# Odd column counts in the additions of 1e-9, 80 partitions of queries and keys for nine heads, and values in one run a partition

## The chip, the cores and the metric

The kernel runs on one core of a Trainium2 chip. The metric is the device time of one execution in microseconds (us), over several runs; the profile is of one execution. The engines are TensorE (PE; PEld is its weight load), VectorE (DVE), ScalarE (ACT), GpSimd (POOL) and SyncE (SP), which issues nearly all DMA transfers here.

## What is computed

Blockwise causal attention of 4 batches, 8 heads, 576 positions and 64 columns a head (block 64), and on its result two feed-forward layers of 2304 tokens, 512 columns and 2048 hidden columns:

```python
scores = scale * np.matmul(q, k.transpose(0, 1, 3, 2))
mask = block_i >= block_j
scores = np.where(mask, scores, -1000000000.0)
scores = scores - np.max(scores, axis=-1, keepdims=True)
attn = np.exp(scores)
attn = attn / (np.sum(attn, axis=-1, keepdims=True) + 1e-09)
x = np.matmul(attn, v)                    # heads side by side: 2304 x 512
h = np.maximum(x @ w_in, 0.0);  x = h * h @ w_out
h = x @ w_in2                             # second layer
g = (a[0] + a[1]*h + a[2]*h**2 + a[3]*h**3) / (1 + abs(b[0])*abs(h) + abs(b[1])*h**2 + 1e-6)
out = g @ w_out2
```

## The kernel before

**Stages.** The program has one attention stage (some 355 us) with the first half of the first layer interleaved into it, then the second half of the first layer, then the second layer. Everything that the change touches lies in the attention stage. A head's 576 queries, padded to 640, are five tiles of 128 rows, in groups `GROUPS = ((0, 1), (2,), (3,), (4,))`. Heads 0 to 7 are visited twice, first for groups 0 and 1 (tiles 0 to 2), then for groups 2 and 3; the other 24 heads once for all four. Each (visit, group) is a slot. The loop at L589 goes through the slots and emits, for slot i: scores (`emit_s`, PE), the normalisation of slot i-1 (`emit_norm`), row maxima (`emit_max`, DVE), exponentials with row sums (`emit_exp`, ACT), the product with the values of slot i-4 (`emit_pv`), the transposes of slot i-3 (`emit_t`, PE, then copies by ACT and DVE), and pieces of the first layer (`moe_a`, through `advance`). Weight conversions (`Converter`, L89 to L129: ACT, DVE and POOL) are put between slots at a fixed pace. The tile framework tracks dependencies and orders the instructions of each engine with a planner that has costs of its own (`schedule_with_timeline_sim=True`, L891); the order in the trace therefore differs a little from the order of the text.

**Plain and split heads.** Heads 0 to 9 are plain (`PLAIN = 10`): they run in float32. The others are split into a high and a low part in float32r. A plain head's query and key arrays have 128 rows: rows 0 to 63 are the transposed head, rows 64 to 68 carry one mark for each tile, by which the score matmul adds the mask, and the rest are zeros. For a split head rows 64 to 127 repeat the head.

**Loads.** `load_qk` (L195) issues one query and one key transfer for each visit (two each for the first), up to four visits ahead; `qr` and `kr` have two buffers. `prep_qk` (L235) scales a plain head's queries on POOL (L239). `make_two` (L214), called at slot 36 with head 9's visit, copies rows 64 to 127 of its query and key tiles. `load_v` (L221) loads the values; two plain heads share a tile `vs` of 5 blocks of 128 columns, the even head in columns 0 to 63 of each block and the odd one in 64 to 127, so a transfer writes runs of 64 numbers (256 bytes) in each partition.

**Normalisation.** The row sums of plain heads lie in `sums`, a tile with two planes of two heads and 8 columns. After the odd head's group 1 (tiles 0 to 2) and group 3 (tiles 3 and 4) DVE adds 1e-9 (L351) for both heads at once, inverts (L352), and POOL spreads the result over 64 columns a head (`rb`, L355); PE transposes that (L447) and DVE multiplies (L449). For the split heads each slot has a tile `stat` (one of 8, 8 columns): negated maxima in columns 0 and 1, sums in 2 and 3, sums plus 1e-9 from 4 on (L362), inverses from 6 on (L363), and POOL multiplies the exponentials by them (L367). In the very first visit the maxima are scaled too (L331).

Of the kernel before, what the change touches and what calls it, by code (L numbers as in the profile page):

```python
# [8 lines left out]
F32 = mybir.dt.float32  # L9
# [3 lines left out]
ALU = mybir.AluOpType  # L13
# [4 lines left out]
P = 128  # L18
S = 576
SP = 640  # L20
D = 64
# [6 lines left out]
NB = 12  # L28
SCALE = 0.125
PLAIN = 10  # L30
SUBS = ((0, 320), (320, S))
SUB = 320
BLK = 512
# [16 lines left out]
def attention_moe_moe(ctx: ExitStack, tc: tile.TileContext, q, k, v, wi1, wo1, wi2, wo2, a, b, out):  # L50
    nc = tc.nc
# [84 lines left out]
    attn = tc.alloc_tile_pool(name="attn", bufs=1)  # L136
# [49 lines left out]
    class Visit:  # L186
        def __init__(self, n, hd, at, gis):
            self.n, self.hd, self.plain, self.at, self.gis = n, hd, hd < PLAIN, at, gis

            self.scale = SCALE if n == 0 else 1.0  # L190

            self.q0, self.q1 = (0, 3 * P) if gis == (0, 1) else (3 * P, SP) if gis == (2, 3) else (0, SP)
            self.k0, self.k1 = (D, D + SUB) if gis == (0, 1) else (0, S)

    def load_qk(un, eng=nc.sync):  # L195
        if len(un.gis) == 2 and un.n % 4 > 1:

            un.qr = f(attn.tile([P, SP], F32R, tag="qh", name=f"qr{un.n}", bufs=2))
            un.kr = f(attn.tile([P, S], F32R, tag="kk", name=f"kr{un.n}", bufs=2))
        else:  # L200
            un.qr = attn.tile([P, SP], F32, tag="qr", name=f"qr{un.n}", bufs=2)
            un.kr = attn.tile([P, S], F32, tag="kr", name=f"kr{un.n}", bufs=2)

        cuts = ((0, 256, D, 256), (256, un.q1, 256, un.k1)) if un.n == 0 else ((un.q0, un.q1, un.k0, un.k1),)
        for q0, q1, k0, k1 in cuts:
            nc.sync.dma_start(un.qr[:, q0:q1], q[un.hd][:, q0:q1])
            eng.dma_start(un.kr[:, k0:k1], k[un.hd][:, k0:k1])

# [10 lines left out]
    def load_v(un):  # L221
        src = v[un.hd].rearrange("p (c d) -> p c d", d=D)
        if un.plain:
            if un.hd % 2 == 0:
                un.vs = attn.tile([P, 5, P], F32, tag="vs", name=f"vs{un.n}", bufs=2)
            else:
                un.vs = units[un.n - 1].vs
            o = D * (un.hd % 2)
            nv = 3 if un.gis == (0, 1) else 5
            nc.sync.dma_start(un.vs[:, 0:nv, o:o + D], src[:, 0:nv])  # L230
        else:
            un.vr = attn.tile([P, 5, D], F32, tag="vr", name=f"vr{un.hd}", bufs=1)
            nc.sync.dma_start(un.vr, src)

    def prep_qk(un, step):  # L235
        if un.plain:
            if step == 0 and un.scale == 1.0:
                cols = un.qr[:, un.q0:un.q1]
                nc.gpsimd.tensor_scalar(cols, cols, SCALE, 0.0, op0=ALU.mult, op1=ALU.add)  # L239
            return  # L240
        if step == 0:
            hd = un.hd
            un.qh = attn.tile([P, SP], F32R, tag="qh", name=f"qh{hd}", bufs=2)
            un.kk = attn.tile([P, S], F32R, tag="kk", name=f"kk{hd}", bufs=2)
            nc.scalar.activation(un.qh, un.qr, AF.Copy, scale=SCALE)
            nc.scalar.activation(un.kk, un.kr, AF.Copy)
        else:
            un.q2, un.k2 = q_two[un.hd % 2], k_two[un.hd % 2]
            nc.vector.scalar_tensor_tensor(
                un.q2[0:D], un.qr[0:D], SCALE, f(un.qh[0:D]), op0=ALU.mult, op1=ALU.subtract)  # L250
            nc.gpsimd.tensor_tensor(un.kk[D:P], un.kr[D:P], f(un.kk[D:P]), op=ALU.subtract)
            nc.sync.dma_start(f(un.k2[0:D]), f(un.kk[0:D]))
# [11 lines left out]
    BANKS = {"mm": 2, "tp": 3, "sy": 1}  # L264


    sts = [attn.tile([P, 8], F32, name=f"stat{n}") for n in range(8)]
    for st in sts:
        nc.vector.memset(st, 1.0)

# [6 lines left out]
    def emit_s(i):  # L277
        un, gi = slots[i]
        g = GROUPS[gi]

        upper = un.gis == (0, 1)
        if un.hd % 2 and gi == 0 if upper else gi % 2:
            ps = ps1.tile([P, 2, 512], F32, tag="sx", name=f"sx{i}")
            if gi != 3:
                ps = ps[:, 0, :]
        else:
            tag = "mm" if upper and gi == 1 else "sy"
            ps = ps1.tile([P, 512], F32, tag=tag, name=f"sy{i}", bufs=BANKS[tag])
        spsum[i] = ps
        for t in g:  # L290

            cols = slice(P * t, P * (t + 1))
            if un.plain:
                products = [(un.qr[:, cols], un.kr)]
            else:
                products = [(un.qh[:, cols], un.kk), (un.q2[:, cols], un.k2)]
            w_ = P * t + D
            if t == 4:
                parts = [(ps[:, 0, 0:HS], 0, HS), (ps[:, 1, 0:HS], HS, S)]
            else:  # L300
                o = D if t == 1 else 0
                parts = [(ps[:, o:o + w_], D, D + w_)]
            for dst, lo, hi in parts:
                for z, (lhs, rhs) in enumerate(products):
                    last = nc.tensor.matmul(dst, lhs, rhs[:, lo:hi], start=z == 0, stop=z == len(products) - 1)
        marks.append(last)
# [13 lines left out]
    def emit_max(i):  # L320
        g = GROUPS[slots[i][1]]
        st = sts[i % len(sts)]
        stats[i] = st
        for n, t in enumerate(g):
            r = D if t == 0 else 0
            gates["max"] = nc.vector.tensor_reduce(st[r:P, n:n + 1], s_view(i, t), axis=AX.XY if t == 4 else AX.X,
                                    op=ALU.max, negate=True)
        un = slots[i][0]
        n = len(g)
        if un.plain and un.scale != 1.0:  # L330
            nc.vector.tensor_scalar(st[:, 0:n], st[:, 0:n], SCALE, None, op0=ALU.mult)  # L331

    def emit_exp(i):
        st = stats[i]
# [9 lines left out]
    def emit_norm(i):  # L344
        st = stats.pop(i)
        un, gi = slots[i]
        if un.plain:
            if un.hd % 2 and gi % 2:
                sm = sums[un.hd // 2 % 2]
                t0, t1 = TILES[gi // 2]  # L350
                nc.vector.tensor_scalar(sm[:, 1, :, t0:t1], sm[:, 0, :, t0:t1], 1e-9, None, op0=ALU.add)  # L351
                nc.vector.reciprocal(sm[:, 1, :, t0:t1], sm[:, 1, :, t0:t1])  # L352
                rb = attn.tile([P, t1 - t0, P], F32, tag="rb", name=f"rb{un.hd}_{gi}", bufs=2, padded_shape=[P, 3, P])
                for t in range(t0, t1):
# [4 lines left out]
            return  # L359
        g = GROUPS[slots[i][1]]  # L360
        n = len(g)
        nc.vector.tensor_scalar(st[:, 4:4 + n], st[:, 2:2 + n], 1e-9, None, op0=ALU.add)  # L362
        nc.vector.reciprocal(st[:, 6:6 + n], st[:, 4:4 + n])  # L363
        for n, t in enumerate(g):
            r = D if t == 0 else 0
            pv = ptile(slots[i][0], t)[r:P]
            nc.gpsimd.tensor_scalar(pv, pv, st[r:P, 6 + n:7 + n], 0.0, op0=ALU.mult, op1=ALU.add)  # L367

    def emit_t(i):
        nonlocal pt  # L370
# [52 lines left out]
    def emit_pv(un, half):  # L423
# [13 lines left out]
        if un.plain:  # L437
            for i, (c, src, dst, width) in enumerate(PV[half]):
                for n_, o in enumerate((0, D)):
                    nc.tensor.matmul(ps[o:o + D, dst:dst + width], un.vs[:, c, o:o + D],  # L440
                                     un.pt[:, n_, ROW[c], src:src + width],
                                     start=i == 0, stop=i == len(PV[half]) - 1)
            rb = spread.pop((hd, half))
# [451 lines left out]
```

## Time and profile before

| | |
|---|---|
| median of 3 runs | 1028.95 us (1028.33 to 1031.23) |
| profiled execution | 1030.96 us, of which its span, from the first to the last instruction, 1029.1 us |
| busy | PE 97%, PEld 86%, DVE 73%, ACT 71%, POOL 58% |
| mean granted TensorE clock | 0.996 |
| DMA | 106.59 MB in 63895 packets, 104 GB/s on average |

[...] A busy PE is one that has a matmul under way; where an engine stands, the wait is put down to what ended it. A share of the whole span says little about one stage, so the stages are read one by one.

### The profile page before, as it was taken

To read this page: it belongs to the slowest core of one execution; us is meant where nothing else is said; L and a number is where in the kernel's file an instruction comes from. 1 tells how busy PE (TensorE), PEld (TensorE's weight loads), DVE (VectorE), ACT (ScalarE), POOL (GpSimd) and SP (SyncE) were. 2 spreads that over 40 slices of the span, in tenths; PEclk is the share of its full clock that TensorE was granted. 3 is DMA by queue.
4 is the path that set the end of the run, shared out by engine and by line. 5 is a ranking of instruction groups with operands and counts; after the bars stand their busy time and mean duration, and the time that the engine had idled before them with its cause. 6 is when DMAs were issued, how large, how long until landed. Compare 5 with 4: busy or idle time off the path is not lost. (4 is left out here: it accounts for less than half of the span.)

```text
span 1029.1 us, 16981 instructions
## 1 busy us (share of the span) xinstructions
PE 993.8 (97%) x5657; PEld 880.1 (86%) x5657; DVE 754.5 (73%) x1436; ACT 732.1 (71%) x1650; POOL 594.3 (58%) x626
## 2 busy tenths in 40 slices
PE   6999998999999999899999999999999999999997
PEld 4668888999999999899788888887888888899996
DVE  6999588868787756677667765787766866776766
ACT  6798676868887755655465557777777777788775
POOL 4677785868687835531223447767455554755552
PEclk9999998999999999999999999999999999999999
DMA  8857434233323204457765473001101100110000
GB/s 282 251 173 235 117 106 150 75 109 104 118 86 86 74 21 128 164 181 231 234 221 182 136 259 123 1 1 41 42 1 31 41 1 1 32 41 1 31 1 32
DMA packets 63895, 106.59 MB, mean 104 GB/s; under 512 B 16064, under 2 KB 34496, under 8 KB 63808
## 3 DMA queue, kind: packets, MB, share of 16 engines
q1 hardware_dynamic: 63520, 105.34, 32.4%
q8 instruction: 45, 0.74, 0.3%
q14 instruction: 42, 0.34, 0.1%
q10 hardware_dynamic: 288, 0.16, 0.1%
HBM read 79.17 MB, written 23.07 MB: 99 GB/s over the span
## 5 line engine op out<-in xcount | busy, mean ns | idle before, releaser
L826 PE MATMUL yc<-w_co,gc 128*128 128x512 f32 x864 | 211.7, 391 | 2.9 <-ACT gc L786 2.9
L717 PE MATMUL hc<-xc,w_ci 128*128 128x512 f32 (+1 forms) x960 | 211.2, 368 | 0.0
L717 PEld LDWEIGHTS hc<-xc,w_ci 128*128 128x128 f32 x960 | 176.2, 188 | 26.2
L826 PEld LDWEIGHTS yc<-w_co,gc 128*128 128x128 f32 x864 | 161.3, 188 | 35.5 <-ACT gc L786 4.4
L787 POOL TENSOR_TENSOR gc<-t,gc 128x512 fp32r<-128x512 f32 (+1 forms) x78 | 105.1, 1354 | 126.3 <-issue 103.4
L493 PE MATMUL ha<-xt,w_ai 128*128 128x320 f32 (+1 forms) x768 | 123.3, 307 | 0.0
L506 PE MATMUL ya<-ga,w_ao 128*128 128x320 f32 (+1 forms) x768 | 117.7, 300 | 3.6 <-ACT r L519 2.2
L812 POOL TENSOR_TENSOR wq<-wq,ab 128x512 f32<-128x512 f32 (+1 forms) x78 | 96.3, 1235 | 28.4 <-ACT wq L810 28.4
L493 PEld LDWEIGHTS ha<-xt,w_ai 128*128 128x128 f32 x768 | 108.4, 191 | 4.7 <-issue 3.0
L506 PEld LDWEIGHTS ya<-ga,w_ao 128*128 128x128 f32 x768 | 106.4, 189 | 5.6 <-ACT r L519 2.4
L757 PE MATMUL yb<-gb,w_bo 128*128 128x512 f32 (+1 forms) x480 | 106.0, 368 | 2.2 <-DVE yp L762 2.0
L717 PE MATMUL hb<-xb,w_bi 128*128 128x512 f32 (+1 forms) x480 | 105.8, 368 | 0.1
L757 PEld LDWEIGHTS yb<-gb,w_bo 128*128 128x128 f32 x480 | 87.6, 188 | 14.2 <-ACT gb L520 2.4
L813 DVE TENSOR_TENSOR t<-hc,t 128x512 f32<-128x512 f32 (+1 forms) x80 | 50.9, 636 | 65.9 <-ACT t L811 65.9
L786 ACT ACTIVATE gc<-t 128x512 fp32r<-128x512 f32 (+1 forms) x80 | 47.1, 589 | 72.9 <-DVE t L795 72.9
L717 PEld LDWEIGHTS hb<-xb,w_bi 128*128 128x128 f32 x480 | 87.4, 188 | 11.6 <-ACT yo L511 0.5
L367 POOL TENSOR_SCALAR p<-p,stat 64x64 f32<-64x64 f32 (+4 forms) x110 | 61.9, 567 | 37.5 <-DVE stat L363 11.7
L387 PE MATMUL tp<-ident,p 128*128 128x128 f32 x416 | 74.4, 286 | 7.0 <-DVE pt L413 4.1
L793 DVE SCALAR_TENSOR_TENSOR wq<-wq,ab 128x512 f32<-128x512 f32 (+1 forms) x80 | 55.0, 687 | 33.8 <-ACT ab L792 22.7
L413 DVE TENSOR_TENSOR pt<-tp,pt 64x64 fp32r<-64x64 f32 (+2 forms) x198 | 64.1, 343 | 19.5 <-ACT pt L411 16.5
L411 ACT ACTIVATE pt<-tp 64x64 fp32r<-64x64 f32 (+2 forms) x198 | 58.2, 320 | 21.6 <-PE tp L387 18.7
L795 DVE SCALAR_TENSOR_TENSOR t<-t,coef,ab 128x512 f32<-128x512 f32 (+1 forms) x80 | 66.8, 835 | 1.7
(140 smaller groups left out, 2006.3 us busy)
## 6 DMA issues: line engine op xcount, KB each, us to landing
kr<-in_k_dram SPq DMA_DIRECT2D x32, 288.0 KB, 3.8
raw_ci<-in_wi_dram SPq DMA_DIRECT2D x16, 512.0 KB, 4.3
raw_co<-in_wo_dram SPq DMA_DIRECT2D x16, 512.0 KB, 4.1
qr<-in_q_dram SPq DMA_DIRECT2D x24, 320.0 KB, 3.2
raw_ai<-in_wi_dram SPq DMA_DIRECT2D x8, 512.0 KB, 4.9
raw_ao<-in_wo_dram SPq DMA_DIRECT2D x8, 512.0 KB, 4.2
raw_bi<-in_wi_dram SPq DMA_DIRECT2D x8, 512.0 KB, 3.7
raw_bo<-in_wo_dram SPq DMA_DIRECT2D x8, 512.0 KB, 3.9
```

The source lines that it names most:

```text
L367: nc.gpsimd.tensor_scalar(pv, pv, st[r:P, 6 + n:7 + n], 0.0, op0=ALU.mult, op1=ALU.add)
L387: nc.tensor.transpose(ps[:, P * n:P * (n + 1)], pblock(un, t, c), ident)
L411: nc.scalar.activation(high, src, AF.Copy)
L413: nc.vector.tensor_tensor(low_, src, f(high), op=ALU.subtract)
L493: nc.tensor.matmul(ps[:, 0:n], w[:, zw, P * kk:P * (kk + 1)], xt[:, zx, kk, first:end], start=i == 0, stop=i == 3 * KK - 1)
L506: nc.tensor.matmul(ps[:, 0:n], wA["o", m][:, zw, P * c:P * (c + 1)], gs[m][:, zg, 0:n], start=i == 0, stop=i == 3 * HALF - 1)
L717: nc.tensor.matmul(ps[:, 0:n], w[:, zw, P * kk:P * (kk + 1)], xt[:, zx, kk, 0:n], start=i == 0, stop=i == 3 * KK - 1)
L757: nc.tensor.matmul(acc[j, c][:, 0:n], wB["o", m][:, zw, P * c:P * (c + 1)], g[:, zg, 0:n], start=m == 0 and i == 0, stop=last and i == 2)
L787: (nc.vector if u - 2 >= len(units) - END else nc.gpsimd).tensor_tensor(g[:, 1, 0:n], t, f(g[:, 0, 0:n]), op=ALU.subtract)
L795: nc.vector.scalar_tensor_tensor(t, t, a0, r, op0=ALU.add, op1=ALU.mult)
L812: (nc.vector if u >= len(units) - END else nc.gpsimd).tensor_tensor(w, w, ab, op=ALU.mult)
L826: last = nc.tensor.matmul(acc[j, c], g[:, zg, P * c:P * (c + 1)], w3["o", m][:, zw, :], start=m == 0 and i == 0, stop=m == NM - 1 and i == 2)
```

## The change

Four edits, all in the attention stage.

1. Additions of 1e-9 and the first scaling get odd column counts. L351 becomes two instructions of three columns, one for each head of the pair, always the last three columns of the half (0 to 2 or 2 to 4; column 2 is added to twice). L362 covers 2n - 1 columns for a group of n tiles: one for one, three for two; the tile `stat` grows from 8 to 11 columns and the inverses move to column 8. L331 is issued once for each column.
2. Heads 0 to 8 load, scale and use 80 partitions of queries and keys (`kp`) in place of 128. Head 9 keeps 128, since `make_two` reads its upper rows.
3. The values of two plain heads lie one head after the other in `vs`, so that each transfer writes one run of 768 or 1280 bytes in a partition.
4. The matmuls of scores and values follow these layouts.

```diff
--- before.py
+++ after.py
@@ -28,6 +28,7 @@
 NB = 12
 SCALE = 0.125
 PLAIN = 10
+KPLAIN = 80
 SUBS = ((0, 320), (320, S))
 SUB = 320
 BLK = 512
@@ -188,6 +189,7 @@
             self.n, self.hd, self.plain, self.at, self.gis = n, hd, hd < PLAIN, at, gis
 
             self.scale = SCALE if n == 0 else 1.0
+            self.kp = KPLAIN if hd < PLAIN - 1 else P
 
             self.q0, self.q1 = (0, 3 * P) if gis == (0, 1) else (3 * P, SP) if gis == (2, 3) else (0, SP)
             self.k0, self.k1 = (D, D + SUB) if gis == (0, 1) else (0, S)
@@ -203,8 +205,8 @@
 
         cuts = ((0, 256, D, 256), (256, un.q1, 256, un.k1)) if un.n == 0 else ((un.q0, un.q1, un.k0, un.k1),)
         for q0, q1, k0, k1 in cuts:
-            nc.sync.dma_start(un.qr[:, q0:q1], q[un.hd][:, q0:q1])
-            eng.dma_start(un.kr[:, k0:k1], k[un.hd][:, k0:k1])
+            nc.sync.dma_start(un.qr[0:un.kp, q0:q1], q[un.hd][0:un.kp, q0:q1])
+            eng.dma_start(un.kr[0:un.kp, k0:k1], k[un.hd][0:un.kp, k0:k1])
 
 
 
@@ -222,12 +224,11 @@
         src = v[un.hd].rearrange("p (c d) -> p c d", d=D)
         if un.plain:
             if un.hd % 2 == 0:
-                un.vs = attn.tile([P, 5, P], F32, tag="vs", name=f"vs{un.n}", bufs=2)
+                un.vs = attn.tile([P, 2, 5, D], F32, tag="vs", name=f"vs{un.n}", bufs=2)
             else:
                 un.vs = units[un.n - 1].vs
-            o = D * (un.hd % 2)
             nv = 3 if un.gis == (0, 1) else 5
-            nc.sync.dma_start(un.vs[:, 0:nv, o:o + D], src[:, 0:nv])
+            nc.sync.dma_start(un.vs[:, un.hd % 2, 0:nv], src[:, 0:nv])
         else:
             un.vr = attn.tile([P, 5, D], F32, tag="vr", name=f"vr{un.hd}", bufs=1)
             nc.sync.dma_start(un.vr, src)
@@ -235,7 +236,7 @@
     def prep_qk(un, step):
         if un.plain:
             if step == 0 and un.scale == 1.0:
-                cols = un.qr[:, un.q0:un.q1]
+                cols = un.qr[0:un.kp, un.q0:un.q1]
                 nc.gpsimd.tensor_scalar(cols, cols, SCALE, 0.0, op0=ALU.mult, op1=ALU.add)
             return
         if step == 0:
@@ -264,7 +265,7 @@
     BANKS = {"mm": 2, "tp": 3, "sy": 1}
 
 
-    sts = [attn.tile([P, 8], F32, name=f"stat{n}") for n in range(8)]
+    sts = [attn.tile([P, 11], F32, name=f"stat{n}") for n in range(8)]
     for st in sts:
         nc.vector.memset(st, 1.0)
 
@@ -291,7 +292,7 @@
 
             cols = slice(P * t, P * (t + 1))
             if un.plain:
-                products = [(un.qr[:, cols], un.kr)]
+                products = [(un.qr[0:un.kp, cols], un.kr[0:un.kp])]
             else:
                 products = [(un.qh[:, cols], un.kk), (un.q2[:, cols], un.k2)]
             w_ = P * t + D
@@ -328,7 +329,8 @@
         un = slots[i][0]
         n = len(g)
         if un.plain and un.scale != 1.0:
-            nc.vector.tensor_scalar(st[:, 0:n], st[:, 0:n], SCALE, None, op0=ALU.mult)
+            for c in range(n):
+                nc.vector.tensor_scalar(st[:, c:c + 1], st[:, c:c + 1], SCALE, None, op0=ALU.mult)
 
     def emit_exp(i):
         st = stats[i]
@@ -348,7 +350,8 @@
             if un.hd % 2 and gi % 2:
                 sm = sums[un.hd // 2 % 2]
                 t0, t1 = TILES[gi // 2]
-                nc.vector.tensor_scalar(sm[:, 1, :, t0:t1], sm[:, 0, :, t0:t1], 1e-9, None, op0=ALU.add)
+                for n_ in range(2):
+                    nc.vector.tensor_scalar(sm[:, 1, n_, t1 - 3:t1], sm[:, 0, n_, t1 - 3:t1], 1e-9, None, op0=ALU.add)
                 nc.vector.reciprocal(sm[:, 1, :, t0:t1], sm[:, 1, :, t0:t1])
                 rb = attn.tile([P, t1 - t0, P], F32, tag="rb", name=f"rb{un.hd}_{gi}", bufs=2, padded_shape=[P, 3, P])
                 for t in range(t0, t1):
@@ -359,12 +362,13 @@
             return
         g = GROUPS[slots[i][1]]
         n = len(g)
-        nc.vector.tensor_scalar(st[:, 4:4 + n], st[:, 2:2 + n], 1e-9, None, op0=ALU.add)
-        nc.vector.reciprocal(st[:, 6:6 + n], st[:, 4:4 + n])
+        w_ = 2 * n - 1
+        nc.vector.tensor_scalar(st[:, 5:5 + w_], st[:, 2:2 + w_], 1e-9, None, op0=ALU.add)
+        nc.vector.reciprocal(st[:, 8:8 + n], st[:, 5:5 + n])
         for n, t in enumerate(g):
             r = D if t == 0 else 0
             pv = ptile(slots[i][0], t)[r:P]
-            nc.gpsimd.tensor_scalar(pv, pv, st[r:P, 6 + n:7 + n], 0.0, op0=ALU.mult, op1=ALU.add)
+            nc.gpsimd.tensor_scalar(pv, pv, st[r:P, 8 + n:9 + n], 0.0, op0=ALU.mult, op1=ALU.add)
 
     def emit_t(i):
         nonlocal pt
@@ -437,7 +441,7 @@
         if un.plain:
             for i, (c, src, dst, width) in enumerate(PV[half]):
                 for n_, o in enumerate((0, D)):
-                    nc.tensor.matmul(ps[o:o + D, dst:dst + width], un.vs[:, c, o:o + D],
+                    nc.tensor.matmul(ps[o:o + D, dst:dst + width], un.vs[:, n_, c],
                                      un.pt[:, n_, ROW[c], src:src + width],
                                      start=i == 0, stop=i == len(PV[half]) - 1)
             rb = spread.pop((hd, half))
```

## Rows read from the trace of the kernel before

**Rows 1.** Page, busy us, share of the span and instructions of each engine.
```profile
PE 993.8 (97%) x5657; PEld 880.1 (86%) x5657; DVE 754.5 (73%) x1436; ACT 732.1 (71%) x1650; POOL 594.3 (58%) x626
```

**Rows 2.** Stages: length, busy PE, PEld, DVE, ACT, POOL, clock, DMA share, GB/s.
```profile
0.00:25.00 25.00, 17.11 (x85) 12.13 (x86) 15.66 (x53) 16.81 (x60) 11.57 (x32) 1.00 0.89 280
25.00:100.00 75.00, 70.09 (x427) 53.16 (x424) 70.03 (x120) 63.19 (x184) 52.54 (x67) 1.00 0.72 220
100.00:360.00 260.00, 252.07 (x1920) 244.63 (x1919) 199.22 (x585) 198.47 (x603) 195.30 (x269) 0.99 0.36 104
```

**Rows 3.** PE's waits, 0 to 25 us: us in total, times, longest.
```profile
PE sy L305 <- DMA kr<-in_k_dram: 3.7, 1, 3.7
PE sx L305 <- DMA kr<-in_k_dram: 1.5, 1, 1.5
```

**Rows 4.** PE's waits, 100 to 360 us.
```profile
PE tp L387 <- DVE pt L413: 3.7, 4, 2.7
...
PE pv L453 <- DVE pt L413: 1.0, 1, 1.0
```

**Rows 5.** DVE groups by form, whole span: busy us, mean ns | idle before.
```profile
L362 DVE TENSOR_SCALAR stat<-stat 128x1 f32<-128x1 f32 x66 | 9.8, 149 | 12.4 <-ACT p L339 11.3 <-ACT ga L520 0.2
...
L362 DVE TENSOR_SCALAR stat<-stat 128x2 f32<-128x2 f32 x22 | 8.6, 390 | 8.9 <-ACT p L339 8.8
...
L351 DVE TENSOR_SCALAR sums<-sums 128x6 f32<-128x6 f32 x5 | 2.8, 560 | 0.0
...
L351 DVE TENSOR_SCALAR sums<-sums 128x4 f32<-128x4 f32 x5 | 1.1, 215 | 0.4 <-ACT p L339 0.4
...
L331 DVE TENSOR_SCALAR stat<-stat 128x2 f32<-128x2 f32 x1 | 0.5, 475 | 0.0
...
L331 DVE TENSOR_SCALAR stat<-stat 128x1 f32<-128x1 f32 x1 | 0.2, 154 | 0.0
```

**Rows 6.** In order of time, from 86.5 us: start, us, engine, line, operation [idle before].
```profile
86.80 1.69 POOL L251 TENSOR_TENSOR kk<-kr,kk 64x576 fp32r<-64x576 f32 x1 [2.55 <-ACT kk L246]
...
87.14 1.38 DVE L351 TENSOR_SCALAR sums<-sums 128x6 f32<-128x6 f32 x1
```

**Rows 7.** In order of time, the first 30 us.
```profile
2.13 0.43 SPq L207 DMA_DIRECT2D kr<-in_k_dram  x1
...
5.71 0.51 POOL L239 TENSOR_SCALAR qr<-qr 128x384 f32<-128x384 f32 x1 [3.00 <-DMA qr<-in_q_dram]
5.77 0.47 DVE L331 TENSOR_SCALAR stat<-stat 128x2 f32<-128x2 f32 x1
...
7.64 1.41 PE L305 MATMUL sx<-kr,qr 128*128 128x64 f32 x4 [1.48 <-DMA kr<-in_k_dram]
```

**Rows 8.** In order of time, from 165 to 176 us.
```profile
167.79 0.15 DVE L362 TENSOR_SCALAR stat<-stat 128x2 f32<-128x2 f32 x1
...
175.22 0.47 PE L387 MATMUL tp<-ident,p 128*128 128x128 f32 x1 [2.65 <-DVE pt L413]
```

**Rows 9.** PE groups by form, 0 to 105 us.
```profile
L305 PE MATMUL sy<-kr,qr 128*128 128x320 f32 x16 | 6.8, 510 | 0.0
...
L305 PE MATMUL sy<-kr,qr 128*128 128x64 f32 x12 | 2.4, 286 | 4.0 <-DMA kr<-in_k_dram 3.7 <-issue 0.3
```

**Rows 10.** Stretches with the k_two copy alone, and with early loads; columns as rows 2.
```profile
139.20:140.00 0.80, 0.80 (x9) 0.80 (x8) 0.80 (x2) 0.80 (x4) 0.80 (x1) 1.00 0.80 184
3.00:5.00 2.00, 1.31 (x5) 1.34 (x6) 0.00 (x0) 0.00 (x0) 0.00 (x0) 1.00 0.73 179
9.00:12.00 3.00, 3.00 (x15) 2.30 (x14) 2.33 (x7) 2.15 (x10) 0.51 (x1) 1.00 1.06 386
```

**Rows 11.** Page, DMA packets of the whole span.
```profile
DMA packets 63895, 106.59 MB, mean 104 GB/s; under 512 B 16064, under 2 KB 34496, under 8 KB 63808
```

**Rows 12.** The stretch of the lower clock; columns as rows 2.
```profile
174.00:183.00 9.00, 7.76 (x37) 7.50 (x38) 6.81 (x25) 4.26 (x15) 2.47 (x5) 0.62 0.54 188
```

## Prediction

> **What bounds the kernel now.** I read the page's busy times first: TensorE (PE) is busy 993.8 of 1029.1 us [rows 1], so no edit can win more than the 35 us in which it stands, and only where it stands. The busy times by stage [rows 2] show where: 7.9 us in the first 25, 4.9 in the next 75, 7.9 from 100 to 360. The reader is to see two things there. From 25 to 100 VectorE (DVE) is as full as PE (70.0 and 70.1 of 75 us), so what DVE does there can delay PE. From 100 to 360 DVE has 61 us free, and extra DVE time mostly fills idle time. The first 25 us are neither.
>
> Who ended PE's waits says what they are. At the start they are mainly two loads, 3.7 and 1.5 us [rows 3]. From 100 to 360 PE waits 4.7 us for DVE in five waits, 2.7 us of it in one [rows 4].
>
> The page and the windows are of one execution, of 1030.96 us with a span of 1029.1, so 1.9 us lie around the span. The median of the runs shown is 1028.95, 2.0 lower. I sum against the execution and carry the difference over to the median.
>
> **The additions.** In one-column form L362 takes 149 ns (66 times), in two-column form 390 (22 times). The sums at L351 average 560 ns with six columns and 215 with four; L331 takes 475 with two and 154 with one [rows 5]. The excess is not work. The six-column addition at 87.14 ends at 88.52, 0.03 us after GpSimd's (POOL's) L251 ends at 88.49 [rows 6]; the two-column L331 at 5.77 ends at 6.24, POOL's L239 at 6.22 [rows 7]. So an operation with an even number of columns waits for the POOL instruction that is running. With POOL idle it does not, as L362 at 167.79 with 150 ns shows [rows 8].
>
> After the change L362 has three columns (or one), L351 is two instructions of three, L331 two of one. No row has an odd count above one. The bounds are the one-column rows (149 ns) and the even rows of the same line (L351: 3.9 us over 10, 390 ns; L362: 390). I take the free price, because only even counts are slow in the rows, but only just; the other is a rival. Then:
> - L362: 22 x (390 - 149) = 5.3 us of DVE saved from 100 on. On the path that is between 0 and the 4.7 us that PE waits for DVE there [rows 4]. Without the one long wait, before which the last two-column addition already takes 150 ns [rows 8], 2.0 are left; I take half, 1.0.
> - L351: 3.9 us now, 20 x 0.149 = 3.0 after, 0.9 saved. It belongs to the plain heads, so to the stage up to 100, where DVE is full; but PE is idle only 4.9 us there [rows 2], and I count half a microsecond for each of DVE's: 0.45. If they wait: 20 x 0.39 = 7.8, so 3.9 lost.
> - L331: 0.63 us becomes 3 x 0.149 = 0.45. I count nothing, since PE's next matmul waits for a load until 7.64 [rows 7]. Where that load is early, 0.2.
>
> The addition of the second half now also rewrites column 2, which the first half's rb copies (L355 on POOL) read. That is a new wait of DVE for POOL, behind which every later DVE instruction would queue. It costs nothing while those copies are two slots old; if they are late, one POOL instruction.
>
> [...]
>
> **Queries and keys, 80 rows.** The number of transfers stays, and none is moved on SP's queue; three eighths of the bytes of the first nine heads go. For each of eight heads that is 768 KB before, for head 8 it is 608: 6752 x 3/8 = 2532 KB, 2.6 MB. Scaling L239 on POOL (0.51 us, [rows 7]) and the score matmuls keep their columns. A matmul's time goes with its columns, 510 ns for 320 and 286 for 64 [rows 9]; no row has fewer contraction rows, so the bounds are 0 and 3/8 of each, and I take 0.
>
> What of the loads is on the path? PE stands 1.48 us until the second unit's keys, issued at 2.13, have landed at about 7.6 [rows 7]. That much can be won there and no more, because the third unit's loads are queued right behind. Of the 3.7 before the first matmul [rows 3] only a small part is transfer: 224 KB at the 386 GB/s of 9 to 12 us [rows 10] are 0.6 us, 3/8 of that 0.2. Bounds 0 to 1.5 and 0 to 0.2; I take 0.7 and 0.2. Later loads are hidden by the matmuls of the units before them: PE names no load after the second unit [rows 3]. Without that cover a key load of 288 KB would give 108 KB at 386 GB/s, 0.3 us.
>
> Against it speaks a transfer of 64 rows in this trace, the k_two copy: alone it moved 184 GB/s with the DMA engines 0.80 busy, while full-height loads from 9 to 12 us moved 386 at 1.06 [rows 10]. Per byte 64 rows cost 1.6 times the engine time, so half the rows cost 0.8 of it, and 80 rows save a fifth at most. For it speaks that the first loads move only 179 GB/s from 3 to 5 us [rows 10]: there the engines' rate is not the limit, and five rows for each of them end sooner than eight. So I take half of the bound.
>
> [...]
>
> **Values.** The 18 loads have 8 x 384 + 10 x 640 = 9472 packets of 256 bytes, of the 16064 that are under 512 [rows 11]; after the change they are 18 x 128 = 2304 larger ones. That frees DMA time, but no wait in rows 3 names a value load: 0, at most 0.2 for the queries behind them.
>
> **Sum.** 0.2 + 0.7 + 0.45 + 1.0 = 2.35 us: 1028.6 against the profiled execution, 1026.6 against the median.
>
> **Rivals.**
> - *The loads don't shrink.* For it the 64-row copy, against it the slow first loads [rows 10]. Then 0.45 + 1.0 are left: 1027.5.
> - *Three columns still wait.* For it every slow row has two columns or more, against it none is odd [rows 5]. L351 loses between 10 x 0.149 = 1.5 and 3.9, say 2.7, half of it on the path; L362 wins 0, the loads 0.9: 0.45 slower, 1029.4.
> [...]
> [...]
>
> **How the numbers follow.** A measurement of this kernel can tell some 0.3% from no change, 3.1 us: under 1025.9 is faster, over 1032.0 slower. Chances: forecast 0.36 (its own range 1024.5 to 1028.6), no shrinking 0.14, still waiting 0.22, stall gone 0.16, new stall 0.12. Faster: 0.14 of the forecast, 0.04, 0.02 and 0.16, together 0.36. Slower: 0.11 of the new stall and 0.03 of the waiting case, 0.14. Same 0.50. The range runs from 1021.0, through the case without the stall, to 1031.5, which takes in the full 3.9 us of waiting sums; the new stall and half of the case without the old one lie outside, 0.2.
>
> **What would show it.** L362 in three columns at 150 ns, and twenty L351 at 150, confirm the first step; 390 refutes it. The second unit's matmul before 7.6 confirms the load term; an unchanged start refutes it. 104.0 MB and some 6600 packets under 512 bytes show that the edits act. [...]

## The result and the profile after

| | before | after |
|---|---|---|
| median | 1029.12 us (1027.62 to 1031.23) | 1039.07 us (1038.10 to 1042.24) |
| ratio | | 1.0099, 95% interval 1.0080 to 1.0117 |
| profiled execution, span | 1030.96, 1029.1 us | 1038.99, 1037.2 us |
| mean granted TensorE clock | 0.996 | 0.993 |

The change makes the kernel 10 us slower, and 1026.6 was forecast. Ratios, here and below, compare runs in the fast state alone; one run of a later kernel, `e1_full_rows` with 2507.41 us, was not in it. The page of the changed kernel has busy times and packets, to be read beside [rows 1, 11]; then come the stages of [rows 2] with the same columns (length, busy PE, PEld, DVE, ACT, POOL, the granted share of TensorE's full clock, the mean busy share of the 16 DMA engines, GB/s).

```profile
PE 1003.4 (97%) x5657; PEld 886.7 (85%) x5657; DVE 756.7 (73%) x1447; ACT 732.8 (71%) x1650; POOL 593.5 (57%) x626
...
DMA packets 55000, 104.00 MB, mean 100 GB/s; under 512 B 6593, under 2 KB 26081, under 8 KB 54913
```

```profile
0.00:25.00 25.00, 21.51 (x77) 16.18 (x77) 15.51 (x52) 14.97 (x53) 10.12 (x33) 1.00 0.76 228
25.00:100.00 75.00, 67.80 (x380) 48.54 (x381) 63.44 (x115) 59.44 (x175) 44.50 (x59) 0.95 0.57 178
100.00:360.00 260.00, 249.58 (x1888) 241.98 (x1886) 202.79 (x582) 198.08 (x599) 194.78 (x263) 0.99 0.37 109
```

TensorE is busy 9.6 us longer with the same 5657 matmuls, and it does fewer of them early: 77 in the first 25 us where there were 85 [rows 2], though it is busy 21.5 us and not 17.1. Matmuls became slower, not more. The loads did what the diff says (104.0 MB, 6593 small packets).

Where the slowness lies is read from one form of matmul in two stretches, the first up to 22 us, the second behind it (busy us, mean ns | idle before).

```profile
L306 PE MATMUL sy<-kr,qr 80*128 80x320 f32 x11 | 6.8, 714 | 0.0
L391 PE MATMUL tp<-ident,p 128*128 128x128 f32 x12 | 3.2, 426 | 0.0
```

```profile
L306 PE MATMUL sy<-kr,qr 80*128 80x320 f32 x6 | 2.2, 452 | 1.6 <-ACT p L341 1.6
L391 PE MATMUL tp<-ident,p 128*128 128x128 f32 x8 | 1.2, 273 | 0.0
```

The same forms take 1.6 times as long before 22 us, the transposes too, which the change does not touch. That is a lower clock level, and the trace's records of the granted clock say the same: their first entry of the full level (1.00) is at 10.7 us before and at 22.0 after. The level up to 22 us is that of the stretch below, 0.50: 192 columns of the product with the values (L444) take 541 ns from 3 to 22 us and 541 ns from 28.9 to 35.5. (The views by stretch print 1.00 ahead of that first entry, so there the durations have to be read.) And the clock falls once more, from 28.8 to 35.6:

```profile
22.00:28.80 6.80, 4.60 (x25) 3.00 (x23) 5.25 (x12) 3.49 (x13) 4.31 (x8) 1.00 0.59 160
28.80:35.60 6.80, 6.28 (x21) 3.76 (x20) 5.02 (x9) 4.93 (x19) 2.29 (x4) 0.50 0.54 156
```

Before that fall TensorE stood 2.2 of 6.8 us. Its longest wait there can be followed back in order of time (start, us, engine, line):

```profile
24.02 2.50 DVE L123 SCALAR_TENSOR_TENSOR cv_ai<-cv_ai,raw_ai 128x512 uint32<-128x512 uint32 x1
...
26.44 0.48 DVE L327 TENSOR_REDUCE stat<-sy 128x1 f32<-128x320 f32 x1
...
26.96 0.53 ACT L341 ACTIVATE p<-sy,stat 128x320 f32<-128x320 f32 x1 [1.83 <-DVE stat L327]
...
27.63 0.81 PE L306 MATMUL sy<-kr,qr 80*128 80x320 f32 x2 [1.62 <-ACT p L341]
```

A conversion of 2.50 us on DVE delays a row maximum, that the exponential, that TensorE.

As a milestone I take the first matmul of the first feed-forward layer, the same instruction in every kernel: at 38.66 us before and at 46.13 after, 7.5 later. Where these 7.5 us come from is seen by the exponentials (each tile of scores has one, in the same order in both kernels). The 5th starts 2.4 us earlier than before (7.82 instead of 10.19 us), the 17th 1.0 us later (24.61 instead of 23.61), the 28th 6.8 us later (45.82 instead of 38.99). So the slow start eats the lead that the loads had given and one microsecond more, and most of the loss at the milestone comes behind it, in and after the half-clock stretch from 28.8. 10.3 us are lost at the layer's 151st matmul (120.97 instead of 110.65 us), 8.0 at the last matmul of the kernel.

### The profile page after: what moved, and what is told of

It reads as the page before. It is cut to its first block, busy times and chain, and to the rows that moved or that the text cites. A ratio compares the mean times of both kernels' runs of the same rounds, so it can differ in the third digit from the quotient of the medians.

```text
span 1037.2 us, 16996 instructions
## 1 busy us (share of the span) xinstructions
PE 1003.4 (97%) x5657; PEld 886.7 (85%) x5657; DVE 756.7 (73%) x1447; ACT 732.8 (71%) x1650; POOL 593.5 (57%) x626
## 2 busy tenths in 40 slices
DMA packets 55000, 104.00 MB, mean 100 GB/s; under 512 B 6593, under 2 KB 26081, under 8 KB 54913
## 5 line engine op out<-in xcount | busy, mean ns | idle before, releaser
L830 PEld LDWEIGHTS yc<-w_co,gc 128*128 128x128 f32 x864 | 161.3, 188 | 35.6 <-ACT gc L790 4.5
L816 POOL TENSOR_TENSOR wq<-wq,ab 128x512 f32<-128x512 f32 (+1 forms) x78 | 96.4, 1236 | 28.7 <-ACT wq L814 28.6
```

The lines of the kernel that those rows point to most:

```text
L816: (nc.vector if u >= len(units) - END else nc.gpsimd).tensor_tensor(w, w, ab, op=ALU.mult)
L830: last = nc.tensor.matmul(acc[j, c], g[:, zg, P * c:P * (c + 1)], w3["o", m][:, zw, :], start=m == 0 and i == 0, stop=m == NM - 1 and i == 2)
```

## The experiments

Theory 1: score matmuls of 80 rows keep TensorE at its lower clock. Theory 2: the earlier loads, or the new order that the planner makes of everything, cost the time. Theory 3: the additions do. The table has all kernels; the clock columns come from the records of the granted clock in each trace, the milestone from its instructions. Each ratio is to the kernel before in runs on the same chip, where its median was 1028.63 to 1029.82 us; it need not be the quotient of two medians. Clock and milestone are of one profiled execution of each kernel.

| kernel | score rows | median us | ratio, 95% interval | full clock first at | half again, up to 100 us | milestone |
|---|---|---|---|---|---|---|
| before | 128 | 1029.12 | 1 | 10.7 | none | 38.66 |
| after | 80 | 1039.07 | 1.0099 (1.0080 to 1.0117) | 22.0 | 28.8 to 35.6 | 46.13 |
| e1_full_rows | 128 | 1028.78 | 0.9992 (0.9973 to 1.0010) | 10.9 | 96.2 to 103.0 | 36.30 |
| e2_matmul_rows | 80 | 1039.16 | 1.0069 (1.0033 to 1.0105) | 38.0 | none | 46.93 |
| e3_edit2 | 80 | 1030.61 | 1.0012 (0.9987 to 1.0036) | 22.0 | 73.2 to 76.6 | 39.22 |
| e4_load_rows | 128 | 1029.11 | 0.9994 (0.9975 to 1.0013) | 6.8 | 10.2 to 17.0, 34.1 to 37.5 | 41.83 |
| text_before | 128 | 1059.58 | 1.0306 (1.0279 to 1.0333) | 12.1 | none | 38.99 |
| text_matmul | 80 | 1067.64 | 1.0379 (1.0362 to 1.0396) | 23.9 | 27.3 to 34.1 | 46.10 |
| text_after_full | 128 | 1060.92 | 1.0314 (1.0292 to 1.0336) | 10.3 | none | 38.42 |
| text_after | 80 | 1063.23 | 1.0336 (1.0318 to 1.0355) | 23.6 | none | 43.80 |
| matmul_96 | 96 | 1031.40 | 1.0024 (1.0011 to 1.0037) | 12.2 | 25.8 to 32.6 | 40.34 |
| single_columns | 128 | 1025.65 | 0.9974 (0.9956 to 0.9993) | 10.9 | none | 38.16 |
| combined | 128 | 1030.46 | 1.0016 (1.0003 to 1.0030) | 7.7 | 28.2 to 31.6 | 38.20 |
| combined_warm | 128 | 1028.86 | 1.0002 (0.9989 to 1.0015) | 5.9 | none | 34.92 |
| after_old_additions | 80 | 1039.56 | 1.0096 (1.0071 to 1.0121) | 21.7 | 28.6 to 35.4, 76.3 to 79.8 | 46.44 |
| after_old_values | 80 | 1034.95 | 1.0058 (1.0035 to 1.0081) | 13.8 | 37.7 to 41.1 | 39.11 |
| after_warm | 80 | 1049.26 | 1.0193 (1.0168 to 1.0218) | 6.1 | four stretches | 49.41 |
| single_warm | 128 | 1029.86 | 1.0013 (1.0001 to 1.0025) | 6.4 | 67.9 to 71.3 | 36.56 |

### The change taken apart

**All but the rows.** The changed kernel with 128 rows:

```diff
-KPLAIN = 80
+KPLAIN = 128
```

> The changed kernel with its 80 rows set back to 128: loads, scalings of the queries and score matmuls of the first nine heads are of 128 rows again, the three-column additions and the values in one run stay. Theory 1 (score matmuls of 80 rows keep TensorE at its lower clock): the granted clock reaches full at about 10 to 11 us, as in the kernel before, the only later stretch at half is the one near 175 us, and the time is 1028 to 1031 us. Theory 2 (the changed order or the earlier loads keep it low): the loads are those of before, so 1028 to 1031 us as well if the loads do it, but about 1038 us if the order that comes with the additions does it. Theory 3 (the additions, which wait beside GpSimd as before and are twice as many in the running sums): 1037 to 1040 us.

The loss is gone: 1028.78 us. Its 128x320 matmuls between 11 and 22 us are at full clock:

```profile
L306 PE MATMUL sy<-kr,qr 128*128 128x320 f32 x10 | 3.6, 439 | 0.0
```

So theory 3 falls: additions and values cost nothing that shows here. The clock did not do all that theory 1 expected: besides the stretch near 175 us it is at half from 96.2 to 103.0 us and twice behind 250 us, and the time is that of the kernel before all the same.

**The matmuls alone.** On the kernel before:

```diff
-                products = [(un.qr[:, cols], un.kr)]
+                products = [(un.qr[0:un.kp, cols], un.kr[0:un.kp])]
```

> The kernel before with one thing changed: the score matmuls of the first nine heads read 80 rows of queries and keys instead of 128 (loads, scalings, additions and values as before). Theory 1: the granted clock is at half until 18 us or later and falls again within the first 40 us; the time is 1036 to 1041 us. Theories 2 and 3: the clock rises at about 10 to 11 us and the time stays at 1027 to 1031 us. The prediction's own term for this step was 0 us.

1039.16 us, by the ratio 7 us (3 to 11) more than before. The fall expected within 40 us did not come, since the clock first rises at 38.0. From 12 to 38 us TensorE has not a gap, and its matmuls still take the time of the lower level (first the two stretches, columns as in the stages above, then a form from 12 to 38 us):

```profile
12.00:38.00 26.00, 26.00 (x83) 17.52 (x82) 13.76 (x38) 16.29 (x60) 12.11 (x22) 1.00 0.73 212
38.00:50.00 12.00, 11.30 (x58) 7.17 (x57) 10.41 (x20) 9.68 (x31) 8.59 (x13) 1.00 0.73 227
```

```profile
L307 PE MATMUL sy<-kr,qr 80*128 80x320 f32 x12 | 7.6, 741 | 0.0
```

So busy time alone did not bring the full level here: TensorE was busy for 26.00 of 26.00 us, and a score matmul of 320 columns still took 741 ns, where `e1_full_rows` above has 439 at the full level.

**The whole of edit 2, and the loads alone.** `e3_edit2` is the kernel before with the diff's loads, scaling and score matmuls of 80 rows. `e4_load_rows` loads 96 rows but keeps matmuls of 128, over rows that VectorE has set to zero:

```diff
+                nc.vector.memset(t[96:P], 0.0)
+                nc.vector.memset(u[96:P], 0.0)
```

> The kernel before with the whole of the second edit: loads, scalings and score matmuls of 80 rows for the first nine heads; additions and values as before. Theory 1: as with the matmuls alone, less the microsecond that the earlier loads give: 1035 to 1040 us, full clock first after 18 us or later. Theory 2 (the loads): the same, so that only the kernels with the matmuls alone and with the loads alone tell these two apart. Theory 3 (additions): 1027 to 1030 us.

> The kernel before with short loads alone: 96 rows of queries and keys are loaded for the first nine heads, rows 96 to 127 of the four pairs of buffers are set to zero once by VectorE, and the score matmuls keep 128 rows. Theory 1: the granted clock reaches full at 9 to 12 us and the time is that of the kernel before or 1 to 2 us less, 1026 to 1029.5 us. Theory 2 (loads that land sooner put the work into an order that keeps the clock low): 1035 us or more. The prediction's load terms (0.2 + 0.7 us) are seen here alone: second unit's first score matmul before 7.2 us instead of 7.64.

The loads alone change nothing in the time that can be measured (0.9994), as theory 1 has it. The second unit's first matmul comes at 5.62 us, as expected (before 7.2), but the eight settings to zero (4.5 us of DVE up to 6.4 us) put the first exponential at 8.26 us instead of 6.34, so what the loads are worth in time is not seen alone here. The clock is full at 6.8 us, sooner than expected, and lost again at 10.2 behind a wait of 2.1 us. The second edit whole was a miss of theory 1: full clock at 22.0 us, as in the changed kernel, and yet 1030.61 us. In its trace no fall follows the rise before 73.2 us, and the 28th exponential starts at 39.57 us where the kernel before has it at 38.99 and the changed kernel at 45.82. From 25 to 100 us VectorE is nearly full in the kernel before (70.0 of 75 us [rows 2]), so TensorE may be able to make up a late start there, if no second fall comes; no run tests that by itself. With 80 rows the clock comes late; what that costs differs from kernel to kernel. Since every kernel so far also had its own order from the planner, this needed a test in which the order stands still.

### The same order on every engine

The planner is switched off in four kernels, so that each engine runs the order of the text:

```diff
-    with tile.TileContext(nc, schedule_with_timeline_sim=True) as tc:
+    with tile.TileContext(nc, schedule_with_timeline_sim=False) as tc:
```

`text_before` and `text_matmul` (the matmul edit above) then have instruction for instruction the same order on all engines, as have `text_after_full` and `text_after`.

> The kernel before with its planner switched off: each engine runs its instructions in the order of the text. It is the baseline of three more kernels with the same order, so that a difference between them is not one of order. Its own time is not known; no theory names it, and somewhat more than 1029 us is likely. What counts is its granted clock in the first 60 us: with score matmuls of 128 rows theory 1 expects full clock from 10 to 13 us.

> The same order of the text, with the score matmuls of the first nine heads reading 80 rows: every engine has the same instructions in the same order as in the baseline, and only these matmuls differ. Theory 1 (the rows keep the clock low): full clock later than in the baseline by 8 us or more, and a time 3 to 10 us above it. Theory 2 (the new order of the planner is what cost the time): the clock as in the baseline and a time within 2 us of it.

> The changed kernel in the order of the text, with its 80 rows set back to 128: against the baseline it has the additions and the layout of the values alone. Theories 1 and 2: within 2 us of the baseline, since the additions move work of VectorE by less than 4 us in all. Theory 3 (the additions cost the time): 5 us or more above it.

> The changed kernel as it is in the order of the text; its engines have the same instructions in the same order as the kernel with 128 rows beside it, and loads, scalings and score matmuls have 80. Theory 1: full clock later by 8 us or more and 3 to 10 us more than that kernel. Theory 2: no more time than that kernel, since the order is the same and the loads are shorter, 0 to 2 us less.

`text_matmul` takes 8.1 us more than `text_before` (1067.64 against 1059.58, and the intervals of the ratios stay apart). The form of its score matmuls from 12.2 to 23.6 us, first of the baseline, then with 80 rows:

```profile
L305 PE MATMUL sy<-kr,qr 128*128 128x320 f32 x8 | 3.2, 482 | 0.0
...
L305 PE MATMUL sx<-kr,qr 128*128 128x192 f32 x4 | 1.1, 354 | 0.0
```

```profile
L305 PE MATMUL sy<-kr,qr 80*128 80x320 f32 x6 | 3.8, 742 | 0.0
...
L305 PE MATMUL sx<-kr,qr 80*128 80x192 f32 x4 | 1.9, 581 | 0.0
```

And stretches of both, in the same order:

```profile
12.00:24.00 12.00, 9.36 (x55) 6.43 (x54) 10.86 (x27) 10.69 (x41) 8.39 (x14) 1.00 0.77 225
24.00:27.30 3.30, 3.30 (x24) 2.37 (x23) 3.24 (x9) 2.75 (x10) 1.69 (x3) 1.00 0.84 231
27.30:34.10 6.80, 6.15 (x29) 3.27 (x27) 5.92 (x14) 6.69 (x24) 5.87 (x12) 1.00 0.76 213
```

```profile
12.00:24.00 12.00, 12.00 (x41) 8.17 (x40) 6.63 (x16) 6.09 (x22) 4.74 (x7) 1.00 0.52 163
24.00:27.30 3.30, 1.66 (x11) 1.12 (x9) 2.84 (x7) 3.20 (x14) 2.22 (x3) 1.00 0.39 79
27.30:34.10 6.80, 6.24 (x20) 4.32 (x20) 4.66 (x12) 3.90 (x15) 3.44 (x7) 0.50 0.70 240
```

From 12 to 24 us the baseline does 55 matmuls in 9.36 us; the kernel with 80 rows does 41 and is busy for all 12.00. It loses 4.9 us there (at the 13th exponential), 2.3 more in the half-clock stretch behind it (at the 20th), and is 7.1 us late at the milestone. Theory 2 can't explain that: nothing in the order differs. In these two kernels the difference shrinks to 5.1 us at the end of the attention and grows to 9.3 in the second layer by further half-clock stretches; those I don't ascribe to the rows. So of the 8.1 us some 5 can be followed to the start; whether the rest belongs to the rows is open.

The fall at 27.3 us stands beside a wait of TensorE for a scaling of queries on POOL (L239): 2.20 us, ended at 27.86. The kernel with 128 rows has the same wait at the same instruction, 2.21 us, ended at 22.95, and stays at full clock.

`text_after` agrees on the clock (23.6 against 10.3 us) and at the milestone (5.4 us later than `text_after_full`), but no fall follows its rise, and its median is only 2.3 us above, short of the 3 expected; the intervals of these two overlap.

### How many rows, one addition, and what is left

`matmul_96` reads 96 rows (the matmul edit with 96), `single_columns` takes the wait out of the split heads' addition:

```diff
-        nc.vector.tensor_scalar(st[:, 4:4 + n], st[:, 2:2 + n], 1e-9, None, op0=ALU.add)
+        for c in range(n):
+            nc.vector.tensor_scalar(st[:, 4 + c:5 + c], st[:, 2 + c:3 + c], 1e-9, None, op0=ALU.add)
```

> The kernel before with the score matmuls of the first nine heads reading 96 rows instead of 128 (80 cost 7 us). If the loss grows with the rows left out, 96 rows lose less than 80: full clock between 11 and 24 us and 1029 to 1036 us. If it is a matter of any missing row, about 1036 us.

> The kernel before with the two-column addition of 1e-9 to the sums of the split heads (390 ns) issued as two additions of one column, nothing else. This measures the prediction's second term alone, 1.0 us of gain: the single columns at about 150 ns each, 300 in place of 390 a slot, and a time of 1027 to 1030 us. A rival: two instructions take DVE as much as one that waits, and the time stays within 0.5 us of the kernel before.

With 96 rows 2.5 us are lost (0.24%), less than with 80: the full level comes at 12.2 us, but a half-clock stretch follows at 25.8. The single columns are the one kernel that beats both, 1025.65 us, 0.7 to 4.5 us less than before; 1027 to 1030 was expected. All 110 take the price of one column:

```profile
L363 DVE TENSOR_SCALAR stat<-stat 128x1 f32<-128x1 f32 x110 | 15.9, 149 | 20.6 <-ACT p L339 20.1
```

The longest wait of [rows 4] stays in it, with 2.7 us, so the gain does not come from there. Which waits gave it was not traced further, and the planner's order is another one here too, so that the gain is not shown to be that of the additions alone.

`combined` puts the useful parts together, and `combined_warm` adds work for TensorE ahead of the first load:

```diff
+    warm = attn.tile([P, SUB], F32, tag="tmp", name="warm", bufs=2)
+    nc.vector.memset(warm, 0.0)
+    for n in range(3):
+        ps = ps1.tile([P, 512], F32, tag="mm", name=f"warm{n}", bufs=2)
+        nc.tensor.matmul(ps[:, 0:SUB], warm[:, 0:P], warm, start=True, stop=True)
```

> What the theories leave of the change as useful: loads and scalings of 96 rows for the first nine heads (two pairs of buffers are loaded in full twice, two are set to zero once in rows 96 to 127), score matmuls of 128 rows, values in one run, the additions of the split heads in single columns, the sums of the plain heads as before. Theory 1: full clock at 9 to 12 us, the first exponentials earlier by up to 1 us than in the kernel before, and 1025 to 1029 us. Theory 2 (loads or order cost the time): over 1033 us.

> The same kernel with three matmuls of 128 x 320 zeros by zeros on TensorE before the first scores (from about 1 to 3.3 us, when it stands waiting for the first load); their result is not used. Theory 1, by which the clock follows what TensorE does with full rows: full clock 1 us or more sooner than in the kernel without them, 8 to 10 us, and 0 to 2 us less time. If the start of the clock hangs on the order or on the loads: no earlier, and the same time or 0.3 us more.

`combined` missed in time, 1030.46 us, 0.16% slower than the kernel before. `combined_warm` takes 1.6 us less than `combined`, within what was expected, and as much as the kernel before. The clock rose sooner than expected in both (7.7 and 5.9 us). `combined_warm` reaches the milestone 3.7 us before the kernel before and the end of the attention 7.3 us before it; at the change to the second half of the layer it waits 3.5 us, and the clock falls there:

```profile
PE hb L739 <- ACT yo L533: 3.5, 1, 3.5
```

Of the 7.3 us 2.5 are left there. In this kernel an early full clock is worth what the next stage lets through.

### What brings the rest of the loss

> The changed kernel with the additions and the scaling of before (same column counts as before; the wider tile stays). If the additions bring the loss beyond the second edit's: about 1030 us. If it is the half clock, wherever its stretches fall: 1033 to 1040 us with full clock not before 20 us, and additions of the plain heads back to ten.

> The changed kernel with the values laid out as before, in runs of 256 bytes. If the layout brings the loss beyond the second edit's: about 1030 us. If it is the half clock: 1033 to 1040 us with full clock not before 20 us.

> The changed kernel with three matmuls of 128 x 320 zeros by zeros ahead of the first scores on TensorE. Theory 1 in its strict form, that score matmuls of 80 rows do not hold the clock: full clock at 6 to 10 us and back at half within the next 15, 1031 to 1038 us. If the rows only hinder the first rise: full clock at 6 to 10 us, no fall in the first 60 us, 1026 to 1030 us.

> The kernel before with the additions of the split heads in single columns, which alone gave a ratio of 0.9974, and the same three matmuls ahead of the first scores. Theory 1: full clock at 6 to 9 us instead of 10.9, and 1021 to 1025 us, faster than both kernels. If the early clock is given back where the loads are the limit: within 1 us of the single columns alone, 1024.5 to 1026.5 us.

`after_old_additions` is the changed kernel with the additions and the scaling of before, `after_old_values` with the old layout of values; the two others have the three matmuls shown above. Without its additions the changed kernel is as slow as with them (1039.56), once more against theory 3. With the old values it is 1034.95 (ratio 1.0058 where the change has 1.0099), about 4 us faster than the change; full clock comes at 13.8 us in its profile, not after 20 as expected. Whether the layout does that or the order that goes with it is open.

`after_warm` is the strictest test: the clock is already full when the score matmuls begin. Its stretches:

```profile
6.10:12.90 6.80, 4.71 (x29) 3.76 (x28) 5.25 (x15) 3.66 (x14) 1.03 (x2) 1.00 0.97 274
12.90:23.20 10.30, 8.62 (x29) 4.94 (x27) 5.47 (x15) 6.85 (x26) 4.98 (x10) 0.50 0.50 142
23.20:30.00 6.80, 4.40 (x25) 3.17 (x24) 6.21 (x15) 4.20 (x16) 4.00 (x7) 1.00 0.94 289
30.00:36.80 6.80, 6.61 (x20) 3.81 (x21) 4.62 (x10) 5.18 (x18) 4.02 (x7) 0.50 0.45 92
```

It falls after 6.8 us, comes back 10.3 us later and falls again; ahead of the two falls TensorE stood 2.1 and 2.4 us. The kernel takes 1049.26 us, more than either reading expected. Not all of that is the clock of the start: in the profiled executions it is 3.3 us behind the changed kernel at the milestone and 9.1 at the last matmul, and in between stands a wait at the change to the second half of the layer:

```profile
PE hb L727 <- ACT yo L521: 4.8, 1, 4.8
```

`single_warm`, with 128 rows and the same start, stays at full clock from 6.4 to 67.9 us; its longest wait from there to 30 us is 1.1 us, where `after_warm` has two of 2.1 and 2.2 beside its falls. So the two do not show that the rows alone took the level away. `e3_edit2` keeps it from 22.0 to 73.2 us with 80 rows; `e4_load_rows` and `combined` lose it with 128, at 10.2 and 28.2 us, at waits of 2.1 and 1.9 us. What stands of theory 1 is the rise: without a start of their own the seven kernels with 80 rows all reach the full level later than the eight with 96 or 128. That 80 rows do not hold it is not shown; the one pair with the same order and the same wait, `text_before` and `text_matmul`, speaks for it, `e3_edit2` against it.

`single_warm` takes 1029.86 us (1.0013), outside both ranges: its lead of 3.6 us at the end of the attention is gone at the change to the second half of the layer, by a wait of 3.4 us.

## Why the prediction was wrong

**The step that failed** is the price of the score matmuls: "A matmul's time goes with its columns ..., so the bounds are 0 and 3/8 of each, and I take 0." Taken matmul by matmul it holds: 192 columns take 354 ns at the full level with 80 rows as with 128, and at the lower level 580 or 581. Beside the rows of `text_before` and `text_matmul` above stand these two, of the changed kernel from 22.2 to 28.6 us and of the kernel before from 3 to 10.6 us:

```profile
L306 PE MATMUL sy<-kr,qr 80*128 80x192 f32 x2 | 0.5, 354 | 0.0
...
L305 PE MATMUL sx<-kr,qr 128*128 128x192 f32 x2 | 1.0, 580 | 0.0
```

But both bounds lay on the side of a gain, and no reason excluded a loss. The loss is not in the instruction but in the clock it runs at: full at 13.8 to 38.0 us in the kernels with 80 rows and no start of their own, at 6.8 to 12.2 in those with 96 or 128. With the rows back at 128 the changed kernel takes 1028.78 us. Measured alone the 80 rows cost 8.1 us in a fixed order, of which some 5 can be followed to the late clock, and 7 (3 to 11) with the planner's; together with the shorter loads (`e3_edit2`) they cost nothing that can be measured.

**The clock stretch was known, and looked for in the wrong place.** The kernel before has one, beside a long wait: TensorE stands 2.65 us up to 175.22 us [rows 8], and the granted clock averages 0.62 over 9 us [rows 12], which I estimate at 9 x 0.38 = 3.4 us. These 6.05 us are behind the chances of a stall that goes (0.16) and of a new one (0.12). The prediction did not ask when the clock rises at the start, though [rows 9] mixes fast and slow matmuls of one form in one mean (510 ns, between 741 and 432). The 1.00 of [rows 2] does not show it either: the first record of the full level is at 10.7 us, and the matmuls ahead of it have the durations of the lower one. A new stall has the right sign and part of what came, a wait and a fall behind it, but the fall is at 28.8 us, the time 1039 us and not the 1032.7 to which 6.05 us bring the forecast, and the rows were not among its reasons. The stall of before did not go: the wait is still there, 2.67 us at 186.95 us instead of 2.65 at 175.22.

**Loads: right at the start, and more than forecast.** The first matmul comes 0.56 us earlier (0.2 was forecast), the second unit's at 5.40 instead of 7.64, without its wait of 1.48 (0.7 forecast):

```profile
3.13 2.47 PE L306 MATMUL sy<-kr,qr 80*128 80x64 f32 x6 [3.13 <-DMA kr<-in_k_dram]
...
5.40 1.27 PE L306 MATMUL sx<-kr,qr 80*128 80x64 f32 x4
```

The scatter is large with the same loads: `e1_full_rows`, with 128 rows, has its second unit's matmul at 6.32 us. But the second unit's keys land at 4.54 to 4.92 us in all six kernels that load 80 rows and at 5.85 to 7.55 in all nine that load 128. So the rival "The loads don't shrink" is refuted. No gain is left at the end of the kernel.

**Additions: the rival was right, if not in size.** The forms of the changed kernel, against [rows 5]:

```profile
L366 DVE TENSOR_SCALAR stat<-stat 128x1 f32<-128x1 f32 x66 | 9.8, 149 | 12.1 <-ACT p L341 11.5
L366 DVE TENSOR_SCALAR stat<-stat 128x3 f32<-128x3 f32 x22 | 8.0, 363 | 8.0 <-ACT p L341 7.9
L354 DVE TENSOR_SCALAR sums<-sums 128x3 f32<-128x3 f32 x20 | 5.0, 252 | 7.7 <-ACT p L341 7.3 <-POOL rb L358 0.5
L333 DVE TENSOR_SCALAR stat<-stat 128x1 f32<-128x1 f32 x3 | 0.4, 150 | 0.0
```

Three columns wait like two, 363 ns against 390: of the 22 at L366, 16 take 277 to 701 ns and end 22 to 28 ns behind the end of a POOL instruction; the other six take 147 to 169. The sums of the plain heads went from 3.9 to 5.0 us of DVE, 1.1 lost, less than the 1.5 to 3.9 us that the rival allowed. The step "only even counts are slow in the rows" generalised from one column to all odd counts, and no row of before had an odd count above one to show it: with three columns it does not hold. The term of 1.0 us for L362 did not come in this form. The wait taken out by single columns goes with 2.7 us (0.7 to 4.5), which has 1.0 inside its interval; whether the term was too small is not decided.

**Values: right at nothing or little with 128 rows.** There they and the additions together give 0.9992. With 80 rows the kernel with the old layout is some 4 us faster, for which no cause was found.

**What stays open.** In the changed kernel 6.8 us are lost by the 28th exponential and 10.3 by 121 us. Part of the later loss comes with two waits at full clock, at 109.22 and 104.37 us, that the kernel before does not have:

```profile
PE tp L391 <- DVE xp L453: 1.8, 1, 1.8
PE tp L391 <- DVE sums L355: 1.6, 1, 1.6
```

Whether they follow from the late start or from the planner's other order can't be told, because the planner's order can't be held while the rows change. Open is also why the clock comes late with 80 rows: the runs show that it does, not by what.

## What to carry to other kernels

Ask of every edit to a matmul not only how long it takes but what it does to the clock that the matmuls around it get, and read the clock from the duration of one form over time, not from a mean. Rows of zeros in a contraction can be worth keeping in the matmul: without them it cost 8.1 us here in a fixed order and 7 (3 to 11) with the planner's, though nothing that can be measured together with the shorter loads (`e3_edit2`). Shortening the load alone was harmless here but gave no time (0.9994), so look at what the next stage does with such a gain. Where a planner orders the work, switch it off in both kernels to see an edit by itself.

## What the runs showed of the hardware

- In `e2_matmul_rows` TensorE was busy without a gap from 12 to 38 us and stayed at the lower clock level (741 ns for 320 columns, 439 at the full level in `e1_full_rows`), with score matmuls of 80 rows among transposes of 128; with 96 or 128 rows the level rose by 12.2 us in every kernel, with 80 and no start of their own at 13.8 to 38.0 us (one execution each).
- A matmul costs the same with 80 and 128 rows at one clock level: 354 ns (full) and 580 or 581 ns (half) for 192 columns.
- Three matmuls of zeros ahead of the first load brought the full level to 5.9 to 6.4 us. In the changed kernel it was lost at 12.9 us, behind a wait of 2.1 us, and the kernel was slower than without them, 1049.26 against 1039.07 us; with 128 rows it lasted to 67.9 us or longer.
- Additions of three columns on DVE waited for POOL as those of two did (363 and 390 ns on average), those of one column did not (149 ns).
- Keys of the second unit landed at 4.54 to 4.92 us when 80 rows were loaded, at 5.85 to 7.55 when 128 were.
